# Attention with memory plus a dense block: segment 0 in whole products, V of two tiles first, four banks chosen by the kernel

## The chip, the cores and the metric

The kernel runs on one core of a Trainium2 chip. The metric is the device time of one execution in microseconds, the median of several runs; it was 220.42 us before (3 runs, 219.96 to 220.6). Beside the runs there is one profiled execution, from which every row below is taken.

## The reference

One input `x` of 2048 rows and 512 columns in bf16 is normalised, and goes through two branches whose outputs are added to it:

```python
xn = _layernorm(x, axis=-1)
return x + _A_ref(xn, A_wq, A_wk, A_wv, A_wo, A_beta) + _B_ref(xn, B_w1, B_w2)
```

Branch B is `silu(xn @ w1) @ w2` with 1792 hidden columns. Branch A is attention with 32 heads of 16 columns, in 4 segments of 512 rows. Within a segment it is causal softmax attention; between segments a memory is read and then added to:

```python
for s in range(N):
    logits = jnp.einsum('bhqd,bhkd->bhqk', qs, ks) * scale + mask
    p = _softmax(logits, axis=-1)
    a_dot = jnp.einsum('bhqk,bhkd->bhqd', p, vs)
    pq = phi(qs)
    num = jnp.einsum('bhld,bhde->bhle', pq, M)
    den = jnp.einsum('bhld,bhd->bhl', pq, z)[..., None] + 1e-06
    a_mem = num / den
    o = g * a_mem + (1.0 - g) * a_dot
    outs.append(o)
    pk = phi(ks)
    M = M + jnp.einsum('bhld,bhle->bhde', pk, vs)
    z = z + jnp.einsum('bhld->bhd', pk)
```

`phi(t)` is `t + 1` above zero and `exp(t)` below; `g` is the sigmoid of `beta`. The heads' outputs go through `wo`.

## The kernel before, in words

**An order written out.** The kernel is a list of words, `ORDER`, and a table, `PIECES`, that says what each word emits. The words are emitted one after the other, under a manual schedule, so each engine gets its own instructions in the order of the list; engines are held together by semaphores alone, which the tile framework places from the reads and writes of each tile. A word that depends on an earlier one through a tile waits for it. The numbers in a word are the segment first, then the tile or column block, then the part: `h0.4.2` is part 2 of hidden block 4 of segment 0, `S5` the scores of batch 5.

**The words.** Products on TensorE: `k`, `q`, `v`, `h` (projections and the hidden layer, `dense` and `dense_mm`), `S` (scores), `E` and `O` (weights times V, for even and odd heads, `weigh`), `m` (memory), `s` (its sums), `n` (memory read), `o`, `oc`, `od`, `oh` (the output rows, in whole, half and quarter widths, `out_mm`), `X` (transposes of the normalised rows, `turn_mm`), `busy` (products without use, ahead of the work). What empties a bank ("eviction"): `kv`, `qv`, `vv`, `Ev`, `Ov`, `Xv` copy it on VectorE, `ka`, `qa`, `va`, `Ea`, `Xa` on ScalarE; `ha` is the tanh of a hidden block on ScalarE, and `hv` the product with it on VectorE, which reads the same bank; `mv`, `sv`, `nv`, `st` read a bank on VectorE too. Others read SBUF alone: `fa`, `ga` (exp for phi on ScalarE), `kp`, `fp`, `gp` (GpSimd), `fv`, `gv`, `Om`, `r`, `w`, `zv`, `dv`, `xs`, `Nv` (VectorE). `tb` loads ScalarE's table for exp. `xl`, `z`, `d`, `t`, `XD` issue transfers on SP's queue, `lw` the loads of w2 and wo on ScalarE's.

**Scores and exp.** `S` writes all four banks of one buffer, the psS tile; one instruction on ScalarE takes the exp of 2048 columns from it into one of six Pb tiles, GpSimd masks them, and `E` and `O` read them. There are 72 such batches. The next `S` has to wait for the exp before it.

**The other four banks.** All other products share the four banks of the pool `pp`. `bank()` takes a tile of one bank from the pool each time, with `bufs=4`: a product group gets a tile of its own, and the group that gets the same bank next waits until the tile is released, that is, until all readers of it are done. Only the last two output tiles use the psS banks (`fin`), and there `out_mm` declares that products into one output and the instruction that reads another do not depend on each other, with the reason "the outputs lie in banks of their own".

**Segment 0.** In segment 0 `dense` works out k, q and h in halves: columns 0 to 255 first, over all four blocks of the contraction, and then 256 to 511, with two products to a part. In segment 1 a part is one product 512 wide, in segments 2 and 3 two.

**Narrow products.** `product` emits a product whole or as four of 32 columns each (L338), whichever fits the word that follows; between scores (`S`, tiled in rows) and others TensorE changes over.

**The head.** The list begins with the statistics of the first four row tiles, 44 and 6 products without use, four transposes `X0.1` to `X3.1`, V of tile 0, then k of block 1 and so on up to `S0`.

Of the kernel before, what the change touches and what calls it, by code (L numbers as in the profile page):

```python
# [19 lines left out]
S1 h0.0.0 h0.0.1 h0.0.2 xs10 h0.0.3 v0.3.0 v0.3.1 v0.3.2 v0.3.3 ha0.0 vv0.3 q0.3.0 kp0.2 hv0.0  # L20
S3 h0.3.0 h0.3.1 q0.3.1 q0.3.2 h0.3.2 tanh XD5 h0.3.3 k0.3.0 Nv7 XD7 q0.3.3 qv0.3 k0.3.1 xs8 ha0.3
S4 Nv4 h0.1.0 k0.3.2 h0.1.1 hv0.3 XD4 h0.2.0 h0.2.1 h0.2.2 h0.2.3 ha0.2 xs9 k0.3.3 kv0.3 hv0.2
S7 xs11 xg8.4 v1.2.0 v1.2.1 v1.2.2 v1.2.3 vv1.2 h0.1.2 h0.1.3 ha0.1 E0
S5 h0.4.0 h0.4.1 hv0.1 Ev0 h0.4.2 h0.4.3 v1.1.0 v1.1.1 fv0.2 v1.1.2 v1.3.0 fp0.3 ha0.4 v1.1.3 vv1.1
S11 hv0.4 q1.2.0 q1.2.1 q1.2.2 v1.3.1 kind fa0.1 q1.2.3 qv1.2 v1.3.2 v1.3.3 vv1.3 Nv8 XD8 O0 lw0 kp0.3 fv0.0 Ov0
S6 fa0.3 k1.2.0 k1.2.1 k1.2.2 h0.5.0 h0.5.1 h0.5.2 q1.1.0 h0.5.3 ha0.5 k1.2.3 kv1.2 q1.1.1 q1.1.2 hv0.5
S8 h0.7.0 q1.1.3 qv1.1 h0.6.0 h0.6.1 h0.6.2 h0.6.3 ha0.6 fv0.3 E1 Ev1 k1.0.0
S9 hv0.6 h0.7.1 h0.7.2 h0.7.3 Om0 ha0.7 k1.0.1 k1.0.2 kp1.2 q1.0.0 q1.0.1 q1.0.2 fp0.1 Nv9 XD9 xs12 k1.0.3 kv1.0 kp1.0
S10 h0.8.0 hv0.7 h0.8.1 h0.8.2 h0.8.3 ha0.8 h0.9.0 h0.9.1 q1.0.3 t0.3 Nv10 XD10 h0.9.2 h0.9.3 qv1.0
S13 hv0.8 O1 Ov1 xs15 v1.0.0 v1.0.1 v1.0.2 ha0.9 v1.0.3 vv1.0 h0.10.0 h0.10.1 bmask  # L30
S12 k1.1.0 k1.1.1 k1.1.2 t0.2 k1.1.3 kv1.1 h0.10.2 h0.10.3 ha0.10 hv0.9 h1.0.0 Om1 h1.0.1 h1.0.2
S15 h1.10.0 h1.10.1 h1.10.2 hv0.10 kp1.1 xl0.2 h1.0.3 ha1.0 Nv11 XD11 E2 Ev2 O2 Ov2
S17 h1.10.3 k1.3.0 hv1.0 k1.3.1 k1.3.2 k1.3.3 kv1.3 fp1.3 h0.12.0 h0.12.1 xs14 m0.2 mv0.2 ha1.10 h0.12.2
S21 fv0.1 q1.3.0 q1.3.1 q1.3.2 q1.3.3 qv1.3 h1.3.0 hv1.10 gp1.1 h0.12.3 ha0.12 t0.1 h1.3.1 h1.3.2 t0.0 h1.3.3
S14 hv0.12 k2.2.0 h0.11.0 h0.11.1 k2.2.1 h0.11.2 h0.11.3 xl0.0 h0.13.0 ha1.3
S16 ha0.11 h0.13.1 h0.13.2 kp1.3 h0.13.3 xs13 kv2.2 hv1.3 ha0.13 q2.1.0 q2.1.1 qv2.1 E3
S19 Ev3 h1.11.0 h1.11.1 h1.11.2 h1.11.3 hv0.11 O3 hv0.13 fa1.3 k2.1.0 mw0.2 k2.1.1 Ov3 kv2.1 Om2
S24 h1.8.0 h1.8.1 h1.8.2 h1.8.3 m0.0 mv0.0 q2.3.0 q2.3.1 qv2.3 ha1.8 hv1.8
S18 v2.1.0 v2.1.1 vv2.1 ga1.0 k2.0.0 o0.2.7 oc0.2.5.0 ha1.11 sv0 r0.1 o0.2.4 k2.0.1 kv2.0 xg12.4
S22 fv1.3 v2.2.0 v2.2.1 vv2.2 o0.2.1 ga1.1 gp1.2 o0.2.6 o0.0.3 o0.0.13 od0.2.11.1 hv1.11 r0.2 o0.0.10  # L40
S20 o0.2.0 oc0.0.2.0 r0.3 lw1 o0.2.2 od0.0.0.2 oc0.2.10.1 h1.1.0 h1.1.1 h1.1.2 h1.1.3 kp2.1 E4 r0.0 od0.0.0.1 ha1.1 gate w0 gv1.1 kp2.0 z0.1
S28 o0.0.6 hv1.1 z0.2 o0.0.8 z0.3 o0.0.11 o0.0.5 Ev4 oc0.0.7.1 Om3 z0.0 o0.2.8 o0.0.12 ga1.2 O4 Ov4
S26 q2.0.0 q2.0.1 h1.7.0 h1.7.1 h1.7.2 h1.7.3 gv1.2 ha1.7 qv2.0 oc0.2.10.0 od0.0.0.3 oc0.0.2.1
S23 fp1.2 od0.2.11.3 h1.4.0 hv1.7 h1.4.1 h1.4.2 Nv14 o0.2.12 h1.4.3 ha1.4 od0.2.11.0 oc0.0.7.0 zv0.3 h1.9.0 o0.2.13 h1.9.1
S25 h1.9.2 h1.9.3 ha1.9 Nv12 XD12 o0.2.3 oc0.2.5.1 gp1.0 zv0.2 o0.2.16 o0.0.16 hv1.4 zv0.0 XD14 zv0.1 E5 o0.0.17 Ev5 hv1.9
S29 fa1.2 o0.2.17 o0.2.14 k2.3.0 gv1.0 k2.3.1 kv2.3 h1.2.0 h1.2.1 h1.2.2
S27 o0.0.9 mw0.0 O5 o0.2.15 Ov5 o0.2.9 Nv13 fp1.0 XD13 h1.2.3 ha1.2 od0.2.11.2 fv1.2 st0.2 t1.2 o0.0.14 o0.0.15
S31 o0.0.4 h1.13.0 h1.13.1 h1.13.2 h1.13.3 ha1.13 o0.3.8 Om5 o0.3.11 o0.3.16 hv1.2 o0.3.9
S30 o0.3.14 h1.12.0 h1.12.1 h1.12.2 h1.12.3 t1.3 Nv15 hv1.13 ha1.12 XD15 od0.0.0.0 o0.1.16 od0.1.8.2 o0.1.17 o0.1.12 hv1.12 oc0.1.9.0
S33 o0.0.1 od0.1.8.3 o0.3.1 xl0.1 od0.1.8.0 st0.0 oc0.1.3.0 o0.1.13 oc0.1.3.1 xl0.3 gp1.3 Om4 fa1.0 o0.1.2 E6 o0.1.0  # L50
S32 kp2.3 Ev6 O6 Ov6 o0.3.17 o0.3.13 o0.3.10 o0.1.6 oc0.3.2.1 o0.1.15 m1.2 fa2.0 mv1.2 fv1.0
S35 o0.1.4 q2.2.0 q2.2.1 qv2.2 fp2.0 ga1.3 v2.0.0 v2.0.1
S34 h1.5.0 h1.5.1 o0.1.14 o0.1.11 t1.0 vv2.0 h1.5.2 oc0.3.0.1 xl1.0 gv1.3 fp1.1 h1.5.3 ha1.5 E7
S41 o0.1.7 Ev7 o0.3.12 o0.1.1 hv1.5 O7 v2.3.0 mw1.2 fa1.1 Ov7 v2.3.1 vv2.3 fv1.1 t1.1
S37 o0.3.5 q3.3.0 q3.3.1 Om7 qv3.3 od0.1.8.1 s1 o0.1.5 sv1 r1.2 o0.1.10 oc0.1.9.1 st0.1 r1.0 od0.3.3.2 ga2.3 kp2.2
S36 k3.1.0 k3.1.1 q3.1.0 q3.1.1 qv3.1 r1.3 r1.1 w1 d1.2 z1.1 z1.2 ka3.1 o0.3.4
S40 h1.6.0 h1.6.1 h1.6.2 h1.6.3 fp2.3 h2.8.0 h2.8.1 ha1.6 o0.3.7
S43 oc0.3.0.0 o0.3.6 od0.3.3.0 hv1.6 od0.3.3.1 m1.0 mv1.0 oc0.3.2.0 od0.3.3.3 o0.3.15 st0.3 o1.2.8 ha2.8 o1.2.7 hv2.8 fv2.0 E8 Ev8 gp2.3
S38 o1.2.13 fa2.2 v3.0.0 v3.0.1 Om6 k3.0.0 od1.2.1.1 k3.0.1
# [883 lines left out]
```

## Time and profile before

| | us |
|---|---|
| median of the runs | 220.42 |
| span of the profiled execution | 218.2 |
| TensorE busy | 210.9 |
| VectorE busy | 181.3 |
| ScalarE busy | 184.1 |
| GpSimd busy | 127.4 |
| first scores start | 11.94 |
| last scores start | 189.99 |

The span runs from the first instruction to the last, some 2.2 us less than a run takes. In the groups of instructions each row has the line of the kernel, the engine, the operation, the tile written and the tile read, their shapes, the count, the busy time in us with the mean of one in ns, and then the time for which the engine stood idle just before, with what ended it. In the waits each row is one engine's line, what it waited for, the total in us, how often, and the longest. In the timeline each row has the start and the length in us. A matmul's row ends when its last value has landed, some time after the next may start. In the table of stretches, each engine's busy time stands with its count of instructions, and the granted clock after them.

### The profile page before, as it was taken

The page shows a single profiled execution, that of the slowest core. Times are in us where ns is not written, and L with a number is a line of the kernel's source. Part 1 is how long each engine was busy: PE and PEld are TensorE (multiplying, and loading weights), DVE is VectorE, ACT ScalarE, POOL GpSimd, SP SyncE. Part 2 cuts the span into 40 slices and gives each one's busy share as a digit, 9 for nine tenths or more (in the row PEclk, how much of TensorE's full clock was granted, in tenths as well). Part 3 has the DMA queues.
Part 4 walks back from the last instruction along what each step waited for, and adds up shares of the span by engine and source line. Part 5 has one row for each costly group of instructions (what it writes and reads, how often), then busy time and mean ns, then how long its engine had stood idle before and what let it go on. Part 6 is the DMA issues. An engine that isn't in the chain of part 4 may idle for free.

```text
span 218.2 us, 9267 instructions
## 1 busy us (share of the span) xinstructions
PE 210.9 (97%) x3982; PEld 116.1 (53%) x4006; DVE 181.3 (83%) x370; ACT 184.1 (84%) x173; POOL 127.4 (58%) x203
## 2 busy tenths in 40 slices
PE   7899999999999999999999999999999999999994
PEld 7666656655544544455444545445464544465653
DVE  6899999999799899667979886887979897858844
ACT  3799999999999999999999999999989998942000
POOL 6067676789568984697766436962787473410000
PEclk9999999999999999999999999999999999999999
DMA  6996249322200430541125131420042120412223
GB/s 183 344 375 160 51 125 243 74 53 53 51 5 17 157 71 10 117 95 40 49 67 83 54 97 28 74 77 6 0 132 73 52 73 13 131 32 79 84 66 98
DMA packets 33273, 19.60 MB, mean 90 GB/s; under 512 B 14672, under 2 KB 33232, under 8 KB 33232
## 3 DMA queue, kind: packets, MB, share of 16 engines
q1 hardware_dynamic: 30608, 16.39, 28.7%
q10 hardware_dynamic: 2624, 2.62, 3.8%
q8 instruction: 31, 0.51, 1.0%
q14 instruction: 10, 0.08, 0.1%
...
## 4 chain that ended last, share of the span: by engine, by line
PE 92%; DMA 3%; ACT 2%; issue 1%; SPq 1%; DVE 0%
PE ps L336 26%; PE psO L338 17%; PE ps L338 16%; PE psS L724 11%; PE psO L336 9%; PE psV L791 8%; PE psS L338 4%; DMA wk_sb<-in_A_wk_dram 3%; ACT Pb L730 2%; PE psM L452 1%; SPq L169 0%; SPq L158 0%; PE ps L509 0%; ACT th L492 0%; DVE o_half L668 0%
## 5 line engine op out<-in xcount | busy, mean ns | idle before, releaser
L730 ACT ACTIVATE Pb<-psS 128x2048 bf16<-128x2048 f32 x72 | 135.2, 1878 | 4.7 <-PE psS L724 2.4
L744 POOL TENSOR_SCALAR_AFFINE_SELECT Pb<-Pb 128x512 bf16<-128x512 bf16 (+2 forms) x88 | 62.3, 718 | 22.4 <-ACT Pb L730 19.6
L497 DVE SCALAR_TENSOR_TENSOR hT<-th,ps 128x512 bf16<-128x512 bf16 x56 | 38.0, 682 | 10.1 <-ACT th L492 9.4
L744 POOL TENSOR_SCALAR_AFFINE_SELECT lows<-Pb 64x512 bf16<-64x512 bf16 (+1 forms) x40 | 24.3, 607 | 32.0 <-ACT Pb L730 24.9
L338 PE MATMUL psO<-w_sb,hT 128*32 128x512 bf16 (+2 forms) x696 | 41.4, 321 | 0.0
L336 PE MATMUL ps<-xnT,w_sb 128*128 128x512 bf16 (+1 forms) x177 | 35.9, 330 | 0.2 <-issue 0.2
L492 ACT ACTIVATE th<-ps 128x512 bf16<-128x512 f32 x56 | 33.0, 594 | 3.5 <-PE ps L338 3.1
L338 PEld LDWEIGHTS <-hT 128*32 128x32 bf16 x864 | 21.5, 96 | 14.6 <-issue 3.1
L338 PE MATMUL ps<-xnT,w_sb 128*32 128x512 bf16 (+1 forms) x408 | 24.8, 349 | 0.0
L724 PE MATMUL psS<-qT,k 32*128 32x64 bf16 (+3 forms) x512 | 23.0, 233 | 0.2
L336 PEld LDWEIGHTS <-w_sb 128*128 128x128 bf16 x178 | 16.4, 98 | 11.9 <-issue 1.2
L336 PE MATMUL psO<-w_sb,hT 128*128 128x512 bf16 (+2 forms) x82 | 20.5, 324 | 0.7 <-issue 0.6
L791 PEld LDWEIGHTS <-Vz 128*32 128x32 bf16 x768 | 16.1, 97 | 9.5 <-issue 0.6
L791 PE MATMUL psV<-Pb,Vz 128*32 128x448 bf16 (+7 forms) x512 | 21.0, 286 | 0.0
L724 PEld LDWEIGHTS <-k 32*128 32x128 bf16 x512 | 9.3, 92 | 21.2 <-issue 20.4
L336 PE MATMUL ps<-xnT,wk_sb 128*128 128x256 bf16 (+1 forms) x63 | 14.4, 326 | 0.4 <-DMA wk_sb<-in_A_wk_dram 0.2
L724 PE MATMUL psS<-qT,kT 16*128 16x448 bf16 (+3 forms) x256 | 14.7, 269 | 0.0
L338 PEld LDWEIGHTS <-w_sb 128*32 128x32 bf16 x408 | 10.3, 96 | 6.7 <-issue 1.7
L621 DVE SCALAR_TENSOR_TENSOR o_out<-psO,x_res 128x512 bf16<-128x512 f32 x14 | 9.4, 679 | 5.0 <-PE psO L338 3.9
L336 PEld LDWEIGHTS <-hT 128*128 128x128 bf16 x92 | 8.5, 98 | 9.6 <-issue 2.1
L828 DVE CAST odd<-psV 128x512 bf16<-128x512 f32 x16 | 11.0, 687 | 2.4 <-PE psV L791 2.4
L338 PE MATMUL psO<-wo_sb,oT 128*32 128x512 bf16 x140 | 12.8, 379 | 0.0
...
## 6 DMA issues: line engine op xcount, KB each, us to landing
...
```

The costliest lines, as they stand in the source:

```text
L336: return [nc.tensor.matmul(out, lhsT=lhsT, rhs=rhs, start=start, stop=stop, skip_group_check=True)]
L338: nc.tensor.matmul(out[c : c + 32], lhsT=lhsT[:, c : c + 32], rhs=rhs, start=start, stop=stop, tile_position=(0, c), skip_group_check=True,)
L452: nc.tensor.matmul(psM[32 * g : 32 * g + 32, i, :].rearrange("p (r d) -> p r d", d=DH), lhsT=st["phiK", dt][:, j, 32 * g : 32 * g + 32], r ...
L492: nc.scalar.activation(out=th[:], in_=sts[s]["h", ft][:, :], func=AF.Tanh, scale=0.5)
L497: nc.vector.scalar_tensor_tensor(out=st["hT"][:, ft, :], in0=st.pop(("th", ft))[:], scalar=1.0, in1=st.pop(("h", ft))[:, :], op0=ALU.add, ...
L621: out = nc.vector.scalar_tensor_tensor(out=o_out[:], in0=st.pop(("psO", j)), scalar=0.5, in1=st["x", j][:], op0=ALU.mult, op1=ALU.add)
L724: nc.tensor.matmul(psS[:, g, c : c + q2 - q1], lhsT=keys[rows], rhs=st["qT"][rows, dt, q1:q2], start=True, stop=True, tile_position=(32 * ...
L730: exp = nc.scalar.activation(out=blocks(Pb, b).rearrange("p y g c -> p g y c"), in_=psS[:, :, :].rearrange("p g (y c) -> p g y c", c=BLOCK ...
L744: over[id(Pb)].append(nc.gpsimd.affine_select(out=out, in_=in_, compare_op=ALU.is_ge, fill=0.0, base=base, pattern=[[0, out.shape[1]], [1, ...
L791: nc.tensor.matmul(psV[32 * g : 32 * g + 32, q0 : q0 + nq].rearrange("p (y c) -> p y c", y=weights.shape[2]), lhsT=Vzs[s % 2][:, kt, 4 * d ...
L828: copy(out=odd[:], in_=sts[s].pop(("psV", 1))[:, :])
```

## The change

Four things change together. In segment 0 only the words of k block 1 (`HALVED`) stay in halves; the other k, q and h of that segment are done as in segment 1, one whole product to a part. V of tiles 0 and 1 comes ahead of k, and both are evicted on ScalarE (`va0.0`, `va0.1`, in place of `vv0.0` and `vv0.1`), ahead of the table load. The four banks are one tile now, and `bank()` gives a view of one of its banks, which the string `BANKS` names in the order of the groups. And the list is another one throughout; it has as many words as before (1349), and 4006 products become 3913.

```diff
 ORDER = """
-ones0 ones1 zeros xc0 xd0 xc1 xq0 xi0 Nv0 busy44 xd1 xq1 xc2 busy6 xi1 X0.1 xd2 xq2 Nv1 X1.1 Xa0.1 v0.0.0 v0.0.1 v0.0.2 xs3 xi2 Nv2 xq3 xi3 v0.0.3 X2.1 Xa1.1 k0.1.0 tb Nv3 X3.1 Xv2.1 k0.1.1 Xv3.1 vv0.0 odd omask k0.0.0 k0.0.1 k0.0.2 k0.0.3 ka0.0 fp0.0 q0.0.0 kf0.0 q0.0.1 q0.0.2 q0.0.3 k0.1.2 k0.1.3 q0.2.0 v0.2.0 qa0.0 xs5 ka0.1 kp0.1
+ones0 ones1 zeros xc0 xd0 xc1 xq0 xi0 Nv0 busy44 X0.1 xd1 xq1 xc2 Xa0.1 xi1 Nv1 v0.0.0 v0.0.1 X1.1 xd2 xq2 xc3 Xa1.1 v0.0.2 v0.0.3 xi2 xd3 xq3 Nv2 v0.1.0 v0.1.1 X2.1 xi3 Nv3 va0.0 Xv2.1 v0.1.2 v0.1.3 X3.1 Xv3.1 k0.1.0 k0.1.1 va0.1 tb odd omask v0.2.0 k0.0.0 k0.0.1 k0.0.2 k0.0.3 ka0.0 fp0.0 kf0.0 q0.0.0 q0.0.1 q0.0.2 q0.0.3 qa0.0 k0.2.0 xl0.2 lw0 v0.2.1 v0.2.2 xs6 v0.2.3
...
+S2 h0.0.3 ha0.0 q0.2.0 q0.2.1 fv0.0 q0.2.2 h0.2.0 q0.2.3 qv0.2 h0.2.1 h0.2.2 XD4 h0.2.3
+S4 h0.1.0 v1.2.0 ha0.2 fp0.2 h0.1.1 v1.2.1 h0.1.2 Nv7 XD7 hv0.0 xs15 v1.2.2 v1.2.3 vv1.2 v1.1.0 xs9 h0.1.3 ha0.1 hv0.2 v1.1.1
+S6 v1.1.2 v1.1.3 q1.2.0 vv1.1 q1.2.1 q1.2.2 q1.2.3 fa0.2 fp0.3 qv1.2 E0 Ev0 h0.4.0
...
 """
+
+BANKS = "0123021032320310132031321320212302012032012302120103210320312310231212212112101213323232323323210220323131031011031133131313213203232332130212321231313131331333020201020221111"
...
-    pp = ctx.enter_context(tc.tile_pool(name="pp", bufs=4, space=bass.MemoryType.PSUM))
+    pp = ctx.enter_context(tc.tile_pool(name="pp", bufs=1, space=bass.MemoryType.PSUM))
...
-    def bank(shape, dtype, name):
-        return pp.tile(shape, dtype, name=name, tag="pb")
+    pool = pp.tile([P, 4, L], F32, name="pb")
+    turns = iter(BANKS)
+
+    def bank():
+        return pool[:, int(next(turns)), :]
...
         if part == 0:
-            sts[s][key] = bank([P, L], F32, "ps")
+            sts[s][key] = bank()
...
+    HALVED = {('k',1)}
+
     def dense(s, name, w_sb, i, part):
 
-        if s == 0:
+        if s == 0 and (name, i) in HALVED:
             if part == 0:
-                sts[s][name, i] = bank([P, L], F32, "ps")
+                sts[s][name, i] = bank()
...
-        psM = st["psM", d0] = bank([P, 2, 2 * DH], F32, "psM")
+        psM = st["psM", d0] = bank()[:, 0 : 4 * DH].rearrange("p (i c) -> p i c", i=2)
...
-        psV = st["psV", par] = bank([P, L], F32, "psV")
+        psV = st["psV", par] = bank()
...
-        ptr = xn["ptr", t] = bank([P, DT, n, P], BF16, "ptr")
+        ptr = xn["ptr", t] = bank()[:, 0 : DT * n * P // 2].bitcast(BF16).rearrange(
+            "p (d n c) -> p d n c", d=DT, n=n
+        )
```

`sums_mm`, `n_mm` and `out_mm` take their bank from `bank()` in the same way.

More of the change, by code (lines that the diff above doesn't have):

```diff
@@ L20 @@
[L20 to L59, printed above, removed]
@@ new lines @@
+S1 q0.3.3 k0.3.2 k0.3.3 kv0.3 v0.3.0 q0.1.0 q0.1.1 v0.3.1 q0.1.2 kp0.3 fa0.3 q0.1.3 qv0.1
+S3 v0.3.2 Nv5 v0.3.3 vv0.3 h0.3.0 h0.3.1 h0.3.2 h0.3.3 ha0.3 Nv4 h0.0.0 XD5 Nv6 XD6 qv0.3 h0.0.1 h0.0.2 hv0.3
+S2 h0.0.3 ha0.0 q0.2.0 q0.2.1 fv0.0 q0.2.2 h0.2.0 q0.2.3 qv0.2 h0.2.1 h0.2.2 XD4 h0.2.3
+S4 h0.1.0 v1.2.0 ha0.2 fp0.2 h0.1.1 v1.2.1 h0.1.2 Nv7 XD7 hv0.0 xs15 v1.2.2 v1.2.3 vv1.2 v1.1.0 xs9 h0.1.3 ha0.1 hv0.2 v1.1.1
+S6 v1.1.2 v1.1.3 q1.2.0 vv1.1 q1.2.1 q1.2.2 q1.2.3 fa0.2 fp0.3 qv1.2 E0 Ev0 h0.4.0
@@ new lines @@
+S5 h0.6.0 h0.4.1 hv0.1 h0.4.2 h0.4.3 ha0.4 fv0.2 O0 Ov0 h0.6.1 h0.6.2 hv0.4 fv0.3
+S8 v1.3.0 v1.3.1 h0.6.3 q1.1.0 q1.1.1 ha0.6 Om0 q1.1.2 q1.1.3 qv1.1 h0.5.0 h0.5.1
+S17 hv0.6 v1.3.2 v1.3.3 vv1.3 h0.5.2 h0.5.3 xs11 k1.2.0 k1.2.1 ha0.5 k1.2.2 k1.2.3 kv1.2 tanh xs8 h0.7.0
+S7 E1 Ev1 t0.3 fa0.1 hv0.5 xs10 xg8.4 h0.7.1 h0.7.2 q1.0.0 q1.0.1 q1.0.2 q1.0.3 qv1.0
+S13 h0.7.3 k1.0.0 k1.0.1 h0.9.0 k1.0.2 h0.9.1 h0.9.2 k1.0.3 h0.9.3 kv1.0 fp0.1 kp1.0 ha0.7 Nv11 XD11 hv0.7
+S9 O1 Ov1 Nv9 h0.8.0 h0.8.1 h0.8.2 h0.8.3 ha0.8 ha0.9 Nv10 h0.10.0 h0.10.1 h0.10.2 hv0.8
@@ new lines @@
+S10 v1.0.0 v1.0.1 v1.0.2 hv0.9 v1.0.3 h0.10.3 Nv8 XD9 ha0.10 q1.3.0 vv1.0 q1.3.1 hv0.10 q1.3.2 XD10 h1.0.0 h1.0.1
+S12 t0.2 k1.1.0 k1.1.1 q1.3.3 h1.0.2 qv1.3 k1.1.2 k1.1.3 kv1.1 h0.12.0 h1.0.3 kind ha1.0 h0.12.1
+S11 h1.10.0 h1.10.1 h1.10.2 gp1.1 h1.10.3 E2 ha1.10 XD8 h0.12.2 h0.12.3 hv1.0
+S15 ha0.12 Ev2 m0.2 k1.3.0 k1.3.1 hv1.10 k1.3.2 O2 mv0.2 Ov2 k2.2.0
+S14 k2.2.1 h1.3.0 h1.3.1 hv0.12 h1.3.2 h1.3.3 k1.3.3 bmask fv0.1 kv1.3 gate q2.1.0 ha1.3
+S16 kv2.2 q2.1.1 t0.1 kp1.1 hv1.3 h0.13.0 h0.13.1 h0.13.2 h0.13.3 h0.11.0 h0.11.1 ha0.13 h0.11.2
@@ new lines @@
+S18 qv2.1 E3 t0.0 xl0.1 h0.11.3 ha0.11 q2.3.0 hv0.13 Ev3 q2.3.1 Om2 qv2.3 m0.0
+S19 hv0.11 mv0.0 v2.1.0 O3 Ov3 k2.1.0 k2.1.1 Om3 fp1.3 ga1.1 kv2.1
+S22 v2.1.1 h1.8.0 h1.8.1 h1.8.2 h1.8.3 k2.0.0 h1.11.0 ha1.8 xl0.0 vv2.1 gv1.1
+S20 hv1.8 o0.2.12 od0.2.11.1 oc0.2.5.1 fp1.0 h1.11.1 k2.0.1 h1.11.2 kp1.2 sv0 kv2.0 xs12 h1.11.3 v2.2.0 ha1.11
+S26 r0.3 o0.2.1 hv1.11 v2.2.1 vv2.2 o0.0.4 od0.0.0.1 oc0.0.2.0 oc0.0.7.0 oc0.0.7.1 r0.2 r0.0 o0.0.6 kp1.3 ga1.2 oc0.2.10.1 od0.0.0.0 kp2.1 o0.2.7 od0.2.11.3
+S21 E4 Ev4 od0.2.11.2 o0.0.5 r0.1 oc0.0.2.1 Om1 h1.1.0 h1.1.1 lw1 h1.1.2 h1.1.3 o0.2.0 w0 ha1.1 z0.3 z0.1 z0.2 z0.0 hv1.1
@@ new lines @@
+S35 Ov6 vv2.0 E7 Om6 Ev7 o0.3.13 h1.5.0 h1.5.1 h1.5.2 h1.5.3 gv1.0 ha1.5 oc0.3.2.0 gp1.3 hv1.5 o0.3.11
+S36 o0.1.16 v2.3.0 xl0.3 v2.3.1 vv2.3 O7 ga1.3 o0.3.10 od0.1.8.0 Ov7
+S37 gv1.3 m1.2 o0.1.5 q3.3.0 q3.3.1 qv3.3 fa1.1 od0.3.3.0 o0.1.1 o0.3.15 mv1.2 fp2.0 oc0.1.9.0 xl1.2
+S41 o0.3.14 fv1.1 t1.1 o0.3.6 s1 sv1 r1.3 o0.1.14 kp2.3 h1.6.0 h1.6.1 h1.6.2 h1.6.3 r1.2 ha1.6 o0.3.12
+S44 o0.1.4 hv1.6 h2.8.0 o0.3.17 xl1.1 r1.0 st0.3 fa2.0 o0.1.17 st0.1 q3.1.0 fv2.0 fp2.2 q3.1.1 qv3.1
+S40 r1.1 h2.8.1 ha2.8 h2.11.0 k3.1.0 k3.1.1 fp2.3 w1 ka3.1 m1.0
@@ new lines @@
+S42 h2.11.1 ha2.11 z1.2 d1.2 z1.1 mv1.0 k3.0.0 k3.0.1 z1.3 v3.0.0 hv2.8 kv3.0 E8
+S38 kp3.0 o1.2.0 o1.2.2 v3.0.1 oc1.2.3.1 Ev8 q3.2.0 fa2.3 q3.2.1 od1.2.1.2 hv2.11 dv1.2 d1.3 qv3.2 od1.2.1.1 od1.2.1.3
+S39 mw1.2 oc1.2.11.1 E9 Ev9 v3.3.0 vv3.0 v3.3.1 zv1.2 o1.2.9 va3.3 d1.1 n1.2 nv1.2
+S45 v3.2.0 xl1.0 oc1.2.3.0 fv2.2 gp2.2 fa2.1 v3.2.1 k3.2.0 vv3.2 O8
+S43 Om5 h2.7.0 o1.2.5 Ov8 h2.7.1 ha2.7 q3.0.0 q3.0.1 qv3.0
+S46 o1.2.12 dv1.3 z1.0 k3.2.1 h2.6.0 h2.6.1 ha2.6 hv2.7 o1.0.4 od1.0.1.0 o1.0.12 xl2.1
@@ L505, in sums_mm @@
             return
-        den = sts[s]["den"] = bank([P, L], F32, "ps")
+        den = sts[s]["den"] = bank()
         for dt in range(DT):
@@ L601, in n_mm @@
     def n_mm(s, dt):
-        ps = sts[s]["n", dt] = bank([P, L], F32, "ps")
+        ps = sts[s]["n", dt] = bank()
         product(ps[:, :], Mbfs[(s - 1) % 2][:, dt, :], sts[s]["phiQT"][:, dt, :], True, True)
@@ L637, in out_mm @@
             if s < LAST or j < 2:
-                st["psO", *key] = bank([P, D], F32, "psO")[:, :]
+                st["psO", *key] = bank()
             else:
```

69 lines of the change are left out of this document (37 added, 32 removed).

## The prediction

> **What bounds the kernel now.** I read the page's head first, then the waits, then the timeline.
>
> ```profile
> span 218.2 us, 9267 instructions
> PE 210.9 (97%) x3982; PEld 116.1 (53%) x4006; DVE 181.3 (83%) x370; ACT 184.1 (84%) x173; POOL 127.4 (58%) x203
> ...
> PEclk9999999999999999999999999999999999999999
> ...
> PE 92%; DMA 3%; ACT 2%; issue 1%; SPq 1%; DVE 0%
> ```
>
> TensorE is busy for 97% of the span, at full granted clock, and makes 92% of the chain that ends last. The kernel is as long as its products. The waits view says how seldom TensorE stands for another engine:
>
> ```profile
> PE ptr L845 <- DVE xn_t L315: 0.5, 1, 0.5
> ...
> PE ps L336 <- DMA wk_sb<-in_A_wk_dram: 0.2, 1, 0.2
> ```
>
> These two are in the head, and no row of some size there has a product waiting for VectorE or ScalarE to empty a bank. Evictions take long all the same; they run behind products that go on in other banks:
>
> ```profile
> L730 ACT ACTIVATE Pb<-psS 128x2048 bf16<-128x2048 f32 x72 | 135.2, 1878 | 4.7 <-PE psS L724 2.4
> L497 DVE SCALAR_TENSOR_TENSOR hT<-th,ps 128x512 bf16<-128x512 bf16 x56 | 38.0, 682 | 10.1 <-ACT th L492 9.4
> L492 ACT ACTIVATE th<-ps 128x512 bf16<-128x512 f32 x56 | 33.0, 594 | 3.5 <-PE ps L338 3.1 <-PE ps L336 0.2
> L828 DVE CAST odd<-psV 128x512 bf16<-128x512 f32 x16 | 11.0, 687 | 2.4 <-PE psV L791 2.4
> L399 DVE CAST qT<-ps 128x512 bf16<-128x512 f32 x15 | 10.3, 686 | 2.4 <-PE ps L338 1.5 <-PE ps L336 0.7
> L406 DVE CAST Vz<-ps 128x512 bf16<-128x512 f32 x15 | 10.2, 679 | 1.6 <-PE ps L336 0.8 <-PE ps L338 0.7
> ```
>
> VectorE needs 0.68 to 0.69 us for one bank whatever the source, ScalarE 0.59 for a tanh and 1.88 for an exp. The second limit is the cadence of the scores, all in one buffer:
>
> ```profile
> 11.98 0.37 PE L724 MATMUL psS<-qT,kT 16*128 16x448 bf16 x4
> 12.40 1.88 ACT L730 ACTIVATE Pb<-psS 128x2048 bf16<-128x2048 f32 x1
> 14.18 0.62 ACT L423 ACTIVATE ex<-kT 128x512 bf16<-128x512 bf16 x1
> 14.35 0.40 PE L724 MATMUL psS<-qT,k 32*128 32x64 bf16 x8
> 14.79 1.88 ACT L730 ACTIVATE Pb<-psS 128x2048 bf16<-128x2048 f32 x1
> ```
>
> An exp follows 0.45 us behind its scores, and the next scores start 0.07 behind the exp's end (14.28): no two exps stand closer than some 2.38 us, and the list gives TensorE about that much between scores.
>
> **The change, part by part.** *Whole products in segment 0.* 84 pairs of half-width products become 84 whole ones.
>
> ```profile
> 17.08 1.05 PE L336 MATMUL ps<-xnT,w_sb 128*128 128x256 bf16 x8
> ...
> 186.35 1.03 PE L336 MATMUL ps<-xnT,w_sb 128*128 128x512 bf16 x4
> ```
>
> One product alone shows 0.39 us but the next starts 0.22 behind it (below), so 0.17 of a row is its tail: (1.05-0.17)/8 = 0.110 for a half, (1.03-0.17)/4 = 0.215 for a whole. 84 x (0.220-0.215) = 0.4 us at most; I take 0.3.
>
> *V of tiles 0 and 1 ahead of k.* Eight products of 0.215 us move to where TensorE waits now:
>
> ```profile
> 7.91 0.40 PE L845 MATMUL ptr<-ident,xn_t 128*128 128x128 bf16 x4
> 8.23 1.28 ACT L309 ACT_TABLE_LOAD   x1
> 8.54 0.39 PE L336 MATMUL ps<-xnT,wk_sb 128*128 128x256 bf16 x2 [0.24 <-DMA wk_sb<-in_A_wk_dram]
> ```
>
> Left alone this fills 0.5 to 0.9 us. Against it stand two casts of 0.58 on ScalarE that now go ahead of the exp's table load (1.28), so the first k eviction and the first scores come later; I put the planned gain at 0.5. On SP and on ScalarE's queue the first residual load and the 1792 KB of w2 are issued ahead of the first scores; the input weights are by then through, and I cost this at nothing (a few tenths if x were delayed).
>
> *The list.* By products alone 17 stretches between scores are up to 0.1 us shorter than the 2.38 us that an exp allows; that would cost some 0.7 us more than now, about what the head gains.
>
> *The banks.* Here lies the sum. Before, every bank was a tile of its own. Now `bank()` hands out views of one tile, and what waits for what is worked out tile by tile: `out_mm` already has to declare the outputs in the psS tile free of each other because they "lie in banks of their own"; nothing of the kind is declared for the new tile. The built program shows it: 199 waits of products are for a reader of the four banks, and 191 of those readers read another bank; 104 evictions in turn wait for a product in another bank. Take this piece of the list: `v1.1.3 q1.2.0 vv1.1 q1.2.1 q1.2.2 q1.2.3 qv1.2 E0 Ev0 h0.4.0`. V lies in bank 1, q in 3, E in 2. vv1.1 waits until q1.2.0 is done; q1.2.1 waits for vv1.1, E0 for qv1.2, h0.4.0 for Ev0. Each eviction in the list becomes a point where TensorE drains, the eviction runs, and TensorE starts again; whatever stands behind on TensorE (scores, and through them the exps) waits along. There are 198 such places: 132 with VectorE evictions only (15 of them with scores among them, which are in a tile of their own and don't wait), 66 with one on ScalarE.
>
> The trace has no such stall in full, but each leg of it:
>
> ```profile
> 204.03 0.39 PE L338 MATMUL psO<-w_sb,hT 128*32 128x512 bf16 x4
> 204.24 0.39 PE L338 MATMUL ps<-phiQT,Mbf 128*32 128x512 bf16 x4
> ...
> 8.77 0.39 PE L845 MATMUL ptr<-ident,xn_t 128*128 128x128 bf16 x4
> 9.19 0.42 DVE L851 COPY xnT<-ptr 128x512 bf16<-128x512 bf16 x1 [0.43 <-PE ptr L845]
> ...
> 6.15 0.38 DVE L315 TENSOR_SCALAR xn_t<-x_lo,mv_all,rstd_all 128x512 bf16<-128x512 bf16 x1
> 6.59 0.40 PE L845 MATMUL ptr<-ident,xn_t 128*128 128x128 bf16 x4 [0.52 <-DVE xn_t L315]
> ```
>
> Tail 0.39-0.22 = 0.17; from 9.16 to VectorE's start 0.03; the cast 0.69; from 6.53 to TensorE's start 0.06: 0.95 us for one VectorE eviction. For a tanh 0.17+0.03+0.59+0.06 = 0.85 if ScalarE is free. It isn't where the tanh stands soon behind scores: in `S2 h0.0.3 ha0.0 q0.2.0` the tanh starts after the exp, 2.2 us behind S2. Adding up the products between scores and tanh I find 14 of the 66 places with ScalarE so taken or with two evictions, at 0.85 us more on average.
>
> Sum: 117 x 0.95 = 111.2; 15 x (0.95-0.43 for the scores, 0.33 with 0.1 of change-over) = 7.8; 66 x 0.85 = 56.1; 14 x 0.85 = 11.9. Together 187.0. From it go the waits that these stalls swallow, those of the head and the exp's cadence (some 1.7), and 0.3 for the halves. With stretches of (2.45 + 2.4) = 4.9 us the 2.38 of the exp no longer binds, and neither the planned gain nor the list's tighter stretches count. 218.2 + 187.0 - 2.0 = 403.2 us of span. The runs before have a median 2.2 us above the profiled span (220.42), so 405.
>
> The bounds: below, 0.85 for each of the 198 and nothing for a busy ScalarE, 168-6.5 = 162, hence 380. Above, each of the 66 finds half an exp ahead of it (66 x 0.94 = 62 in place of 11.9), hence 455. I stay at 405, as the placing of each tanh can be read in the list.
>
> **Rivals.** *A: the evictions overlap.* If the waits across banks were met before a product reaches them, only the planned parts would count: -0.5 (head), -0.3 (halves), +0.7 (tight stretches), 220.3 us, and without the last 219.6: not slower. It decides where an eviction ends before the product ahead of it does. For it speaks that today no bank makes TensorE wait; against it that 104 evictions may not start until the product just ahead has ended, so they cannot end before it, and that the scores show a wait kept to 0.07 us. The Trainium skill, "PSUM — Partial Sum Buffer", section on bank collisions, asks for a semaphore only between engines on one bank and quadrant, others run clean side by side; by that rule the chip needs none of these waits and the sum would be A's 220.3. The built program waits nevertheless.
>
> *B: the clock falls too.* The head shows two speeds for equal products:
>
> ```profile
> 1.11 4.74 PE L864 MATMUL psS<-zraw 128*128 128x128 bf16 x50 [1.11 <-DVE zraw L188]
> ...
> 1.00:3.00 2.00, 1.89 (x19) 1.90 (x19) 1.28 (x2) 1.28 (x1) 1.80 (x8) 1.00 0.59 161
> ...
> 4.80:5.50 0.70, 0.70 (x15) 0.70 (x13) 0.66 (x5) 0.03 (x1) 0.00 (x0) 1.00 0.69 228
> ```
>
> Of the 50 idle-time products 19 take 2 us (0.105 each) after the start; later 15 products take 0.7 (0.047), with a granted clock of 1.00 in both. A TensorE idle for half of the time, in pieces of 0.95 us, may drop back to the slow speed. All of its 206 us of products (210.9 busy less those 4.7) at half speed give 405+206 = 611; a quarter of the time 455. For it speaks only that cold start; against it that no idle piece reaches 3 us. The Trainium skill, "TensorE: Matmul & The Clock Gate", Part 1, has the clock fall after one idle window of about 3.4 us, by which it would stay up and 405 hold; its passage on PSUM-queue cycling reports short idles that did make it oscillate, which is B. No run here shows either.
>
> **How the numbers follow.** Forecast 0.82, A 0.05, B beyond a quarter 0.13. Of the forecast's own weight nearly all lies between the bounds, so 380 to 455 holds about 0.8. Slower by over 0.3%, about what a measurement here can tell from no change, comes with the forecast and B: 0.95; A splits into 0.03 faster and 0.02 the same.
>
> **What would show it.** Right: TensorE busy for about half of the span; waits of products for hT, Vz, qT, kT, oraw, odd and th among the longest rows, near 190 us in all; exps some 4.9 us apart; the first scores near 18 us (11.95 now, and seven evictions of 0.85 to 0.95 in the head's list); stalls of 0.95 and 0.85 us one by one. Wrong: TensorE still above 90% busy (A); whole products spaced 0.43 us within a group (B); or stalls well under 0.85 us, which would say that an eviction starts before the product ahead of it ends.

## The result, and the profile after

| | before | after |
|---|---|---|
| median of six runs, us | 220.19 | 493.38 |
| ratio, 95% interval | | 2.2336 [2.2266, 2.2407] |
| span of the profiled execution | 218.2 | 487.6 |
| mean granted clock of TensorE | 1.00 | 0.740 |
| first exp, last exp | 12.40, 190.44 | 18.34, 447.69 |

Two of the six runs of the kernel after (499.46 and 501.11 us, at a clock of 0.71) are in a slower state than the rest; the median holds them, the ratio leaves them out.

The predicted direction came, and the size did not: 405 us was forecast, with 455 as the upper end. First the page of the kernel after, the rows that were shown of before: busy time of the engines, the granted clock in 40 slices, the shares of the chain that ended last.

```profile
span 487.6 us, 9128 instructions
PE 317.2 (65%) x3891; PEld 131.2 (27%) x3913; DVE 184.2 (38%) x368; ACT 189.9 (39%) x175; POOL 122.0 (25%) x203
...
PEclk9985579755956898975565556558797557998899
...
PE 59%; DVE 21%; ACT 11%; issue 7%; another core or an unknown queue 1%; DVEq 0%; ACTq 0%
```

VectorE, ScalarE and GpSimd work as long as before (184.2 for 181.3, 189.9 for 184.1, 122.0 for 127.4 us); the span grew around them. VectorE and ScalarE now make a third of the chain. TensorE is busy for 317.2 us where it was 210.9, though it does 93 products fewer, and the row of the clock, all nines before, falls to five in 14 of the 40 slices. Two things happened, then: TensorE waits, and it runs slowly.

The waits view of the kernel after (waiting engine, line, what for: us in total, times, longest) shows the first:

```profile
ACT Pb L737 <- PE psS L731: 166.4, 62, 7.5
...
PE pb L343 <- DVE hT L504: 23.0, 25, 2.0
PE pb L341 <- DVE hT L504: 19.8, 22, 2.3
PE pb L341 <- ACT th L499: 16.0, 19, 1.5
PE pb L343 <- ACT th L499: 12.1, 15, 1.7
PE pb L343 <- DVE odd L835: 10.1, 12, 1.5
```

Such rows of products behind VectorE or ScalarE, of which before had none of any size, make 164.1 us in 198 waits. The exps in turn wait 166.4 us for scores. Each eviction takes as long as before (columns of the groups: busy us and mean ns, then the idle time ahead of it and its main releaser):

```profile
L504 DVE SCALAR_TENSOR_TENSOR hT<-th,pb 128x512 bf16<-128x512 bf16 x56 | 38.5, 688 | 95.3 <-PE pb L343 48.3
L499 ACT ACTIVATE th<-pb 128x512 bf16<-128x512 f32 x56 | 33.3, 596 | 88.5 <-PE pb L343 42.3
L406 DVE CAST qT<-pb 128x512 bf16<-128x512 f32 x15 | 10.4, 691 | 31.8 <-PE pb L341 26.9
```

A few places in order of time (timeline of the kernel after: start, us, engine, line, operation; in brackets the idle time before it and what ended it):

```profile
129.96 0.69 DVE L406 CAST qT<-pb 128x512 bf16<-128x512 f32 x1 [2.66 <-PE pb L341]
130.30 1.88 ACT L737 ACTIVATE Pb<-psS 128x2048 bf16<-128x2048 f32 x1 [0.81 <-PE psS L731]
130.70 0.73 PE L798 MATMUL pb<-Pb,Vz 128*32 128x512 bf16 x16 [0.45 <-DVE qT L406]
131.25 0.39 PE L343 MATMUL pb<-xnT,w_sb 128*32 128x512 bf16 x4
132.07 0.59 ACT L499 ACTIVATE th<-pb 128x512 bf16<-128x512 f32 x1
132.72 0.61 PE L343 MATMUL pb<-xnT,wq_sb 128*32 128x512 bf16 x8 [1.07 <-ACT th L499]
133.45 0.69 DVE L504 SCALAR_TENSOR_TENSOR hT<-th,pb 128x512 bf16<-128x512 bf16 x1 [2.81 <-PE pb L343]
134.06 0.68 DVE L828 CAST oraw<-pb 128x512 bf16<-128x512 f32 x1
...
134.79 0.79 PE L343 MATMUL pb<-xnT,wq_sb 128*32 128x512 bf16 x8 [1.46 <-DVE oraw L828]
```

The cast of q ends at 130.65, and the even product of another bank starts at 130.70. The tanh of 131.25's product has to wait until the exp is nearly through (132.07, the exp's row ends at 132.18), and q starts 0.06 behind the tanh's end. Then two evictions stand one behind the other on VectorE, and q's next half waits for both. That is the drain of the prediction, one after the other.

The second thing is the clock. The profile states it as a share of full speed, the granted clock. The windows view (stretch, its length, busy us and instructions of PE, PEld, DVE, ACT, POOL, then granted clock, DMA share, GB/s), cut where the clock may change:

```profile
124.90:128.30 3.40, 1.54 (x7) 0.66 (x7) 1.38 (x2) 2.07 (x2) 1.17 (x2) 1.00 0.41 92
128.30:131.70 3.40, 2.16 (x32) 0.72 (x31) 0.69 (x1) 2.00 (x2) 0.64 (x2) 1.00 0.02 5
131.70:135.10 3.40, 0.92 (x16) 0.42 (x16) 1.65 (x3) 0.97 (x2) 1.05 (x2) 1.00 0.00 0
135.10:138.50 3.40, 2.17 (x64) 0.95 (x60) 1.59 (x4) 1.13 (x1) 0.00 (x0) 0.50 0.01 1
138.50:141.90 3.40, 2.61 (x48) 1.37 (x44) 1.54 (x2) 1.26 (x2) 2.37 (x3) 0.50 0.02 5
```

In the window from 131.70 TensorE is busy for 0.92 of 3.40 us, in two pieces with waits of 1.07 and 1.46 us ahead of them; the next window runs at half clock. A row of four whole products from another stretch, where the granted clock is 0.50 as well, shows what that does:

```profile
264.35 1.86 PE L341 MATMUL pb<-xnT,wq_sb 128*128 128x512 bf16 x4 [0.78 <-DVE oraw L828]
```

Before, such a row took 1.03 us. (1.86 - 0.17)/4 = 0.42 us for one product is twice 0.215, the spacing that the prediction had named as the sign of its rival B.

To split the time in two I add up every product of the trace by its columns: 0.215 us for 512 of them (the prediction's spacing), that is 0.42 ns each, twice that where the granted clock is 0.5, overlaps counted once ("streaming" below). What is left up to the last product is idle:

| us | span | streaming | of it at half clock | idle | time at half clock |
|---|---|---|---|---|---|
| before | 218.2 | 189.4 | 0 | 25.7 | 0 |
| after | 487.6 | 263.7 | 153.5 | 220.5 | 253.5 |
| four tiles | 233.7 | 191.3 | 3.4 | 39.0 | 4.4 |
| before, one tile | 485.0 | 264.6 | 155.4 | 217.1 | 249.7 |
| two tiles | 322.0 | 195.3 | 10.2 | 123.3 | 13.7 |
| first product five times | 535.7 | 313.2 | 73.5 | 218.4 | 96.9 |

(The last four rows are experiments below; the last three of them are of one run each.) In each of these traces 22 to 25 products have no row (3982 rows for 4006 weight loads before, 3891 for 3913 after); their streaming, some 5 us, is counted as idle here. As it is nearly the same in every row, the differences hold to a microsecond or two. Of the 269.4 us that the span grew, 194.8 are idle time, and 74.3 streaming: half of 153.5, 76.8 us, is what the half clock added.

### The profile page after: what moved, and what is told of

The parts are those of the page before. It is cut to its first block, busy times and chain, and to the rows that moved or that the text cites. A ratio compares the mean times of both kernels' runs of the same rounds, so it can differ in the third digit from the quotient of the medians.

```text
span 487.6 us, 9128 instructions
## 1 busy us (share of the span) xinstructions
PE 317.2 (65%) x3891; PEld 131.2 (27%) x3913; DVE 184.2 (38%) x368; ACT 189.9 (39%) x175; POOL 122.0 (25%) x203
## 4 chain that ended last, share of the span: by engine, by line
PE 59%; DVE 21%; ACT 11%; issue 7%; another core or an unknown queue 1%; DVEq 0%; ACTq 0%
PE pb L343 24%; PE pb L341 22%; DVE hT L504 7%; ACT th L499 7%; PE pb L798 6%; PE psS L731 4%; ACT Pb L737 3%; DVE odd L835 2%; DVE oraw L828 2%; DVE qT L406 2%; DVE oT L615 2%; DVE Vz L413 2%; DVE kT L383 2%; DVE o_out L628 1%; PE psS L873 1%
## 5 line engine op out<-in xcount | busy, mean ns | idle before, releaser
L737 ACT ACTIVATE Pb<-psS 128x2048 bf16<-128x2048 f32 x72 | 135.2, 1877 | 166.4 <-PE psS L731 166.4
L504 DVE SCALAR_TENSOR_TENSOR hT<-th,pb 128x512 bf16<-128x512 bf16 x56 | 38.5, 688 | 95.3 <-PE pb L343 48.3
L343 PE MATMUL pb<-w_sb,hT 128*32 128x512 bf16 (+2 forms) x644 | 52.7, 384 | 32.9 <-DVE hT L504 11.6
L499 ACT ACTIVATE th<-pb 128x512 bf16<-128x512 f32 x56 | 33.3, 596 | 88.5 <-PE pb L343 42.3
L341 PE MATMUL pb<-xnT,w_sb 128*128 128x512 bf16 x111 | 44.0, 486 | 22.6 <-DVE hT L504 5.7
L343 PE MATMUL pb<-xnT,w_sb 128*32 128x512 bf16 x440 | 42.0, 489 | 15.5 <-DVE hT L504 4.9
L341 PE MATMUL pb<-w_sb,hT 128*128 128x512 bf16 (+2 forms) x98 | 29.7, 386 | 22.0 <-DVE hT L504 7.8
L798 PE MATMUL pb<-Pb,Vz 128*32 128x448 bf16 (+7 forms) x512 | 29.9, 369 | 12.6 <-DVE hT L504 3.6
L341 PE MATMUL pb<-xnT,wq_sb 128*128 128x512 bf16 x44 | 18.4, 508 | 11.0 <-ACT th L499 3.6
L341 PE MATMUL pb<-wv_sb,xnT 128*128 128x512 bf16 x34 | 14.4, 486 | 10.7 <-DVE hT L504 5.1
L343 PE MATMUL pb<-wo_sb,oT 128*32 128x512 bf16 x120 | 13.7, 461 | 9.9 <-DVE hT L504 5.8
```

Of the source, the lines that this page charges most:

```text
L341: return [nc.tensor.matmul(out, lhsT=lhsT, rhs=rhs, start=start, stop=stop, skip_group_check=True)]
L343: nc.tensor.matmul(out[c : c + 32], lhsT=lhsT[:, c : c + 32], rhs=rhs, start=start, stop=stop, tile_position=(0, c), skip_group_check=True,)
L499: nc.scalar.activation(out=th[:], in_=sts[s]["h", ft][:, :], func=AF.Tanh, scale=0.5)
L504: nc.vector.scalar_tensor_tensor(out=st["hT"][:, ft, :], in0=st.pop(("th", ft))[:], scalar=1.0, in1=st.pop(("h", ft))[:, :], op0=ALU.add, ...
L737: exp = nc.scalar.activation(out=blocks(Pb, b).rearrange("p y g c -> p g y c"), in_=psS[:, :, :].rearrange("p g (y c) -> p g y c", c=BLOCK ...
L798: nc.tensor.matmul(psV[32 * g : 32 * g + 32, q0 : q0 + nq].rearrange("p (y c) -> p y c", y=weights.shape[2]), lhsT=Vzs[s % 2][:, kt, 4 * d ...
```

## The experiments

Theory T, formed from this trace: the one tile makes every eviction a point where TensorE drains, and the clock falls because TensorE then streams for too small a share of its time. Against it stand L, that the new list or its choice of banks is slow by itself, and C, that the clock falls with idle pieces as such, whatever the share.

### Four tiles in place of one

```diff
-    pool = pp.tile([P, 4, L], F32, name="pb")
+    pool = [pp.tile([P, L], F32, name=f"pb{i}") for i in range(4)]
 ...
-        return pool[:, int(next(turns)), :]
+        return pool[int(next(turns))][:, :]
```

> The kernel after with one edit: the four banks are four tiles of [128, 512] again, taken in the same order of BANKS; list, whole products and V ahead of k stay. Theory T (the one tile makes every eviction a point where TensorE drains, and the clock falls because TensorE then streams too small a share of its time): no drains, granted clock 1.00, TensorE above 95% busy, 219.0 to 221.0 us. Rival L (the new list or its choice of banks is slow by itself): a good part of the 273 us stays, above 260 us. If only a small part is the list's (the 17 tight stretches between scores), 220.5 to 222.

Measured: 233.72 us, 1.0607 [1.0569, 1.0644] of before. 259.7 of the 273.2 us are gone with the one tile, and the clock is up again; 13 us are not. They are idle time (39.0 for 25.7 us). The page and the waits view of this kernel:

```profile
PE 214.9 (92%) x3891; PEld 107.2 (46%) x3913; DVE 186.2 (80%) x368; ACT 185.5 (79%) x175; POOL 129.4 (55%) x203
...
PEclk9999889999999999999999999999999999999999
```

```profile
PE pb L341 <- DMA xnT<-xn_t: 3.7, 1, 3.7
PE pb L341 <- DVE hT L504: 2.3, 3, 1.3
...
PE pb L459 <- DMA phiK<-pk: 1.5, 1, 1.5
```

No range of the expectation holds 233.72. T is right for the bulk and L for 13 us, more than the "0.7" that I gave the list.

### The kernel before with one tile

The kernel before with its list and its halves, with `bank()` as in the kernel after and a BANKS string that names the banks it has anyway.

> The kernel before with its own list, its halves and its own bank for each product, but the four banks as views of one tile. Counted from the list, 159 pieces of products stand behind a drain against 160 in the kernel after, 140 us of stalls against 141 by the same model. T: 460 to 520 us with a granted clock of 0.65 to 0.85, though nothing of the new list is in it. Rival L: clearly under the kernel after, below 400 us.

Measured: 486.66 us, granted clock 0.743, 217.1 us idle. The one tile alone takes the old list to within 1.4% of the kernel after. L is out for the bulk.

### Two tiles of two banks

```diff
-    pool = pp.tile([P, 4, L], F32, name="pb")
+    pool = [pp.tile([P, 2, L], F32, name=f"pb{i}") for i in range(2)]
 ...
-        return pool[:, int(next(turns)), :]
+        turn = int(next(turns))
+        return pool[turn // 2][:, turn % 2, :]
```

> The kernel after with two tiles of two banks each (banks 0 and 1, banks 2 and 3). The same model counts 102 drains and 72 us of stalls against 160 and 141, so by the 176 us measured in the kernel after some 90 us of stalls here. T: TensorE streams some 0.68 of the time in the mean, so few of the clock's 3.41-us windows fall to 0.38: 305 to 345 us, granted clock 0.88 to 1.00. Rival C (the clock falls with the number of idle pieces of about 1 us, whatever the share): 102/160 of the kernel after's 91 us come too, 360 us or more, clock near 0.8.

Measured: 323.71 us. The view of the cores:

```profile
core 0: 322.0 us, clock 0.979
```

Idle time is 123.3 us, 97.6 more than before, about half of the 194.8 of one tile. But the time at half clock is 13.7 us for 253.5, about a nineteenth. C would have it near half of the 253.5. The clock's price comes all at once, where the share gets low enough.

### More products between the same waits

```diff
-            product(sts[s][key][:, :], lhsT(ki), rhs(ki), ki == 0, ki == DT - 1)
+            for _ in range(5 if ki == 0 else 1):
+                product(sts[s][key][:, :], lhsT(ki), rhs(ki), ki == 0, ki == DT - 1)
```

> The kernel after, one tile, where the first of the four products of each whole k, q, v and h is done five times over (each starts the sum anew, so the result stays); 103 x 4 x 0.215 = 89 us more to stream at full clock, between the same stalls. T: the share rises in the windows that fell (0.22 to 0.38 now), the clock mostly stays up, and the 91 us of streaming at half clock go as the 89 us come: 480 to 530 us, granted clock above 0.88. Rival C (the clock falls with idle pieces whatever the share): the added products run at half clock for half of the time too, 493 + 89 x 1.5 = 625 us, above 590, clock 0.75 or less.

Measured: 537.38 us.

```profile
core 0: 535.7 us, clock 0.910
```

The idle time is the same (218.4 for 220.5 us) in waits of the same places, and the time at half clock falls from 253.5 to 96.9 us. C is out. T's number was too low: 89.5 us of streaming came as worked out, but of the 76.8 us of the half clock only 40.0 went, as 13 windows still fall; 487.6 + 89.5 - 40.0 - 2.1 = 535.0.

With these runs a rule can be read off. The clock changes only at borders 3.41 us apart. I take the share of streaming in each such window, over the kernel after and these four: 410 windows at full clock, 53 of them followed by a fall. A bound at a share of 0.37 puts some 9 of the 410 on the wrong side: nearly all that fall had 0.11 to 0.38, nearly all that stay 0.38 and more. The bound is fitted to these same windows, and a product without a row lowers the share of its window by 0.06, so the second digit is uncertain. Sorted by the longest idle piece that touches the window, the best bound leaves 50 wrong, hardly better than saying that none falls; pieces of 0.94 us do for some falls. The way back needs more: of 180 windows at half clock, the 53 that return lie mostly above 0.71 (17 on the wrong side). In the kernel before no window has less than 0.60.

The Trainium skill, "TensorE: Matmul & The Clock Gate", Part 1, has the clock fall after one idle window of about 3.4 us. The length of the window agrees; an idle window wasn't needed: of the 53 falls one stands behind an idle piece of that length (3.86 us, in the run with four tiles). The same page of the Trainium skill, in its passage on PSUM-queue cycling, reports short idles between groups that make the clock swing; that is what came, with idle pieces from 0.94 us up.

### What the list has left: w2, V ahead, whole products, banks

Four runs on the 13 us. First, with four tiles, w2's issue back to where before has it:

```diff
-... qa0.0 k0.2.0 xl0.2 lw0 v0.2.1 ...
+... qa0.0 k0.2.0 xl0.2 v0.2.1 ...
-... fv0.2 O0 Ov0 h0.6.1 ...
+... fv0.2 O0 lw0 Ov0 h0.6.1 ...
```

> The kernel of the run with four tiles (233.7 us), where the issue of w2's 1792 KB goes back from ahead of the first scores to where the kernel before has it, behind the first odd product O0. There v1.2.0 waits 3.86 us on TensorE for the DMA transposes of x (19.26 to 28.57 us, with the DMA busy for 0.96 of 20 to 25 us; 18.33 to 24.59 in the kernel before), and one clock window falls behind it (granted clock 0.991). Theory W (w2's transfer holds the transposes up): 3.9 + some 2 of the clock come back, 226.5 to 229 us, clock 1.00. Rival L (the transposes stand late in SP's list, or the list is too tight, whatever w2 does): 232 to 234.

Measured: 230.69 us, 1.0492 [1.0461, 1.0522], 3.0 us less than with w2 ahead. Timeline of the run with four tiles:

```profile
19.26 9.31 SPq L866 DMA_TRANSPOSE xnT<-xn_t  x4
...
27.27 0.39 PE L341 MATMUL pb<-wv_sb,xnT 128*128 128x512 bf16 x1 [3.69 <-DMA xnT<-xn_t]
```

And with w2 later:

```profile
19.39 6.17 SPq L866 DMA_TRANSPOSE xnT<-xn_t  x4
...
35.56 0.45 DVE L842 COPY_PREDICATED oraw<-omask,odd 128x256 int32<-128x256 int32 x1 [2.40 <-DMA zraw<-oraw]
35.90 0.68 DVE L406 CAST qT<-pb 128x512 bf16<-128x512 f32 x1
36.64 0.81 PE L341 MATMUL pb<-xnT,wk_sb 128*128 128x512 bf16 x3 [1.79 <-DVE qT L406]
```

The transposes take 6.17 us again as they did before (6.26), and TensorE's wait in front of that product shrinks from 3.69 to 0.35 us: W is right. But less came back than the 226.5 to 229 us expected, because w2 now goes out at 30.22, just behind the small transfers of `E0` (`zraw<-oraw`, issued from 29.57 on): VectorE waits 2.40 us for them with the merge `Om0`, q's eviction stands behind it in VectorE's order, and TensorE waits 1.79. Whether w2 delays those transfers was tested further down.

The same edit the other way round, in the kernel before:

```diff
-... q0.2.0 v0.2.0 qa0.0 xs5 ...
+... q0.2.0 v0.2.0 qa0.0 lw0 xs5 ...
-... O0 lw0 kp0.3 ...
+... O0 kp0.3 ...
```

> The kernel before with one edit: w2's 1792 KB are issued where the kernel after issues them, right behind qa0.0 and ahead of the first scores. W: the transposes of x come some 4 us later here too; the old list first reads them at much the same place (v1.2.0 behind some six scores), so 223 to 227 us with one wait of 2 to 4 us on TensorE. Rival L: no change, 219.8 to 220.8.

Measured: 222.57 us, 1.0110 [1.0090, 1.0130]. The size is W's, nearly, but its place isn't. The transposes hardly suffer (6.87 us); its waits view names the others:

```profile
ACT gate L249 <- DMA beta_r<-in_A_beta_dram: 1.7, 1, 1.7
DVE stats L286 <- DMA x_hi<-in_A_x_dram: 1.0, 1, 1.0
```

beta of 0.2 KB, issued on SP a microsecond ahead of w2 (9.97 and 10.99), comes late, and ScalarE's `gate` waits for it 1.7 us with the exps behind it; x for the statistics comes 1.0 us late on VectorE (at 20.47, where before had no wait). In both lists a reader pays; which one depends on the list.

Whole products alone:

```diff
-        if s == 0:
+        if s == 0 and (name, i) == ("k", 1):
```

> The kernel before with whole products in segment 0 (all but k of tile 1), nothing else. By the prediction's term: 84 x 0.0035 = 0.3 us less, 219.6 to 220.3 us. Rival: a whole product needs all four tiles of x, so k0.0 and q0.0 start later and the first scores with them: 0 to 1 us more.

Measured: 221.12 us, 1.0035 [1.0020, 1.0050]: slower, by the rival. The first exp of before stood at 12.40; in this run's timeline:

```profile
9.92 1.02 PE L336 MATMUL ps<-xnT,wk_sb 128*128 128x512 bf16 x4 [0.29 <-DVE xnT L851]
...
13.08 1.88 ACT L730 ACTIVATE Pb<-psS 128x2048 bf16<-128x2048 f32 x1
```

k of tile 0 can't start until all four tiles of x are turned, and the 72 exps follow the first at their cadence (last exp at 190.99 for 190.44).

The banks in turn, with the new list:

```diff
-    pool = pp.tile([P, 4, L], F32, name="pb")
 ...
-        return pool[:, int(next(turns)), :]
+        return pp.tile([P, L], F32, name="pb", tag="pb")[:, :]
```

(with a pool of four)

> The kernel after with the four banks taken in turn (a pool of four tiles) in place of BANKS; list, whole products and V ahead of k stay. If the choice of banks matters to the new list, products wait for evictions of the next bank in turn: 236 to 250 us. If it doesn't, the same as four tiles with the banks chosen, 233 to 234.5.

Measured: 233.22 us, 1.0590 [1.0549, 1.0630], against 1.0607 [1.0569, 1.0644] with the banks chosen. The choice of banks makes no difference that these runs can tell.

### Longer leads

On the run with the banks in turn: w2 behind `tanh` in S17's line, `m0.0 mv0.0` from the border of S18 and S19 to that of S22 and S20, `Nv15 XD15 Nv13 XD13` from S31's line to S32's, behind `st0.0`.

> The run with the banks in turn (233.2 us), where three things of its list get longer leads: w2 is issued behind tanh in the line of S17 (some 37 us), m0.0 with mv0.0 stands one line later, and the normalized tiles 15 and 13 with their transposes stand one line later, behind st0.0. Theory G (what the list has left over 220 us are products that stand too soon behind a chain over the DMA or GpSimd: v1.2.0 behind the transposes 3.1 us, k1.2.0 behind the shift of odd, m0.0 behind phiK's transpose 1.6, o0.3.8 behind the tiles' rstd 1.5): these three or four waits go, 3.1 + 1.6 + 1.5 and some 1 of the clock, 225.5 to 228 us. Rival L (the list as a whole is tight, so each wait that goes shows up again later): 230 to 233.

Measured: 230.68 us, 1.0446 [1.0404, 1.0488]. That lies within L's bounds, not G's. The waits that were named did go: m0.0's and o0.3.8's, and the 3.1 us for the transposes are 0.3 now. With w2 far from `E0`'s transfers VectorE waits 0.5 us for them, as it does in the run with four tiles, where w2 goes out early, against 2.40 with w2 right behind them: w2 had been in their way. But others stand in their place. VectorE's rows in the waits view:

```profile
DVE phiQT L605 <- DMA spr<-rz: 2.2, 1, 2.2
...
DVE xn_t L317 <- DMA xnT<-xn_t: 1.0, 1, 1.0
```

Behind the first (it ends at 123.78) q's eviction starts at 124.25 and TensorE waits 1.17 us for it; behind the second, V's starts at 46.77 and TensorE waits 1.31 us. It is one mechanism both times: an operation that needs a DMA stands in VectorE's order ahead of an eviction. The idle time is 35.7 us here, 10.0 more than before; what is left of it beside these two, waits of 0.3 to 1.0 us each, was not tried one by one, and whether this mechanism accounts for them too stays open.

### V ahead alone, and whole products where nothing waits

The kernel before with `v0.1.0` to `v0.1.3` and `va0.0`, `va0.1` ahead of the table load, as in the kernel after:

> The kernel before with only V of tiles 0 and 1 moved: the products of V of tile 1 ahead of k, both evictions on ScalarE ahead of the exp's table load; halves, banks and the rest of the list stay. By the prediction's planned gain 0.5 us less, 219.5 to 220. By its doubt (two casts of 0.58 and V's 0.86 us go ahead of the first k eviction, and all 72 exps follow the first at their cadence): the first exp comes 0.3 to 0.7 us later and the end with it, 220.5 to 221.2.

Measured: 221.76 us, 1.0056 [1.0033, 1.0080]: slower, as the doubt had it, and by more than the doubt's 221.2. In its timeline the table load, 8.23 before, and the first exp, 12.40 before:

```profile
9.86 1.28 ACT L309 ACT_TABLE_LOAD   x1
...
13.34 1.88 ACT L730 ACTIVATE Pb<-psS 128x2048 bf16<-128x2048 f32 x1
```

The kernel before with halves kept for what the first scores wait for:

```diff
-        if s == 0:
+        if s == 0 and (name, i) in (("k", 0), ("k", 1), ("q", 0)):
```

> The kernel before with whole products in segment 0 except for k of tiles 0 and 1 and q of tile 0, which the first scores wait for. With all but k of tile 1 whole the first exp came at 13.08 us for 12.40 and the run took 0.8 us more. If the late first scores are that whole loss: the first exp at 12.4 again and 219.9 to 220.5 us, at best the 0.3 us of the prediction's term. If whole products cost by themselves: 220.9 or more.

Measured: 220.55 us, 1.0003 [0.9987, 1.0019]: no difference, first exp at 12.17. So the loss of whole products is the late first scores, and their gain of 0.3 us isn't to be seen. No run here beats the kernel before.

## Why the prediction was wrong, point by point

**The drains: right.** 198 waits of products behind VectorE and ScalarE stand against 198 places counted; that the two agree to the last is partly luck, as one of the waits is for `zraw` at the start, which is no eviction. Their 164.1 us are below the "near 190 us" named as a sign, as the view counts from the end of a product's row and leaves out its tail, 198 x 0.17 = 34 us. Place by place (start of the next product less the end of the last one's streaming) the median is 0.945 us at full clock and 0.988 at half where VectorE alone evicts, for 0.95; 0.44 and 0.68 us with scores among them, for 0.52 (few places, and not sharply told from others in the trace). Where a tanh or cast of ScalarE stands, the median is 0.932 and 0.917 and the mean 1.15 and 0.96, for 0.85 with 0.85 more at 14 places, 1.03 in the mean. The idle time grew by 194.8 us; the sum had 185.0. Without the 13.3 us that stay with four tiles it is 181.5.

**The clock: the step that failed.** The 218.2 us from which the sum set out held every product at full clock, the sum had no term for the clock, and rival B was put down with "no idle piece reaches 3 us". The kernel ran 253.5 us at half clock, 52% of its time, and that made 76.8 us. One idle piece did reach 3 us (3.35 at 109.86), but the other 15 of this kernel's 16 falls came without one. The sum with this term is 218.2 + 185.0 + 76.8 = 480.0 for a span of 487.6. The number against which to weigh B was to be had: drains of 0.95 us between pieces that stream for 0.86 put the share near a half in the mean, and under that wherever a busy ScalarE or two evictions come together. What wasn't to be had from the trace of before is the bound of 0.37, as none of its windows lies below 0.60.

The prediction also misread its sign for B. It took the products of the start, 0.105 us apart, to run at a granted clock of 1.00, like those 0.047 apart behind them. The trace of before has no record of the clock ahead of 4.87 us, and the view shows 1.00 where there is none. At 0.42 ns a column, 128 columns take 0.054 us at full clock and 0.107 at half. So the start fits a half clock, and what it showed was most likely the very slowing that came.

**The range.** Its upper end let every ScalarE eviction find half an exp ahead of it and left the clock at full; B's price "a quarter of the time", 455, closed it. By B's own formula, the 41% of the streaming that ran at half (76.8 of 263.7 - 76.8 = 186.9 us at full speed) gives 405 + 0.41 x 206 = 489; its 206 us are the rows' time, tails and all, where the columns take 186.9.

**The first scores near 18 us: right** (first exp at 18.34). The exps' distance of 4.9 us became 6.05 in the mean, (447.69 - 18.34)/71, with the clock.

**Rival A: 233.7 us, not 220.3.** With the waits across banks gone the planned parts cost 13 us, for these reasons as far as the runs show them. w2 ahead of the first scores was "cost at nothing" since the input weights were through; it costs 1.1%, 2.4 us, in the old list and 3.0 us in the new, because x, beta and the transposes were not through. The gain of 0.5 in the head is a loss of 0.56%, 1.2 us, when V ahead is done alone: the two casts do push the table load back, and the first exp with it, as the prediction's doubt said. The 0.3 of the halves is 0.8 us the other way. If these add up, which was not tried, they make some 5 of the 13 us. The list's tight stretches, priced at 0.7 by their products, are not the rest: with four tiles no scores wait for an exp in TensorE's rows of the waits view. At the two waits followed above, the list puts an operation that needs a DMA too near to an eviction on VectorE, and a count of products between scores doesn't show that; what makes the others stays open.
